# Loading a projection weight to 112 partitions in one DMA in place of two DMAs to 128

## The chip, the cores and the metric

The kernel runs on one core of one Trainium2 chip. The metric is device time in microseconds (us); profiles were taken of the same kernels, one execution each. Executions of the kernels before and after agree within 0.6 us, those of one experiment within 1.5 us.

## The reference, cut to what matters

One token is decoded. Its query comes from a small projection, attends to 65,536 cached positions in each of eight key/value heads, and the result is mixed with a small MLP.

```python
Hq, Hkv, Sk, Dh = 16, 8, 65536, 256      # x: [1, 1, 448], wq: [448, 4096], caches: [1, 8, 65536, 256]
q = (x @ wq)                             # 448 x 4096: 3.67 MB of bf16, the weight that the change is about
scores = einsum("bhqd,bhkd->bhqk", q, k) * Dh ** -0.5
o = einsum("bhqk,bhkd->bhqd", softmax(scores), v)
a = o @ wo
out = g * a + (1 - g) * mlp(x)           # g = sigmoid(sum(x * gate_w))
```

Keys and values are 537 MB; all inputs together, 544 MB. Every byte is read once.

## The kernel before

wq is loaded first, into bytes that the values take over later. 384 of its 448 rows go to 128 partitions of three rows; the other 64 are cut in halves, so that 128 partitions get half a row each.

```python
WF = 3                                   # rows per partition in the first load
REM = DM - WF * P                        # 64 rows left, two half rows each
HALF = NQ // 2
wq_a = early[:, 0:WF * NQ].rearrange("p (j n) -> p j n", j=WF)     # early: the value buffer
wq_b = early[:, WF * NQ:WF * NQ + HALF]
...
# SyncE
eng.dma_start(wq_a..., A_wq[0:WF * P, :].rearrange("(p j) n -> p (j n)", p=P)).then_inc(sem_wq, 16)
eng.dma_start(wq_b, A_wq[WF * P:DM, :].rearrange("r (a n) -> (r a) n", a=2)).then_inc(sem_wq, 16)
for j in range(NP):                      # 32 steps
    if j >= 1: eng.wait_ge(sem_tr[NB - 1], BODY * (j - 1) + DC)    # half of the last keys transposed
    load(kring, A_k_cache, j, ...)       # 8.39 MB of keys
    if j == 0: eng.wait_ge(s_q, 1); eng.wait_ge(s_hb, 1)           # wq and the scratch rows are used up
    else:      eng.wait_ge(sem_pv, j)
    load(vbuf, A_v_cache, j, ...)        # 8.39 MB of values
    ...
# TensorE
for dj in range(2):
    for h in range(HQ):
        for kt in range(WF):
            pe.matmul(sps[:, 1, j:j + 1], wq_a[:, kt, col + dj:col + DH:2], xcol[:, kt:kt + 1], ...)
        ins = pe.matmul(sps[:, 1, j:j + 1], wq_b[:, cb + dj:cb + DH:2], xcol[:, WF + a:WF + a + 1], ...)
```

ScalarE issues the small loads (x, the gate, the MLP's weights and biases) on a queue of its own at the same time.

The softmax here doesn't subtract the row's maximum and nothing guards it: scores larger than these inputs give would overflow.

## Time and profile before

| | before |
|---|---|
| median of three runs | 1266.69 us (1266.55 to 1266.86) |
| span of the profiled run | 1264.3 us |
| bytes read | 544.22 MB, 430 GB/s over the span |
| first packet of the large queue | 1.8 us into the span |
| last landing, end of the last work on it | 1261.53, 1262.2 us |

The views that carry the argument stand in the prediction. One more line of the page is needed for the comparison: the GB/s of the 40 slices of the span, 31.6 us each. The first slice holds the loading stage.

```profile
GB/s 410 428 432 431 435 433 433 431 435 433 431 435 433 433 431 435 431 435 431 435 433 429 433 435 435 431 435 431 431 433 435 435 431 435 431 431 433 435 425 363
```

And the two wq loads among the page's DMA issues; the last number is the time from issue to landing:

```profile
vbuf<-in_A_wq_dram SPq DMA_DIRECT2D x1, 3072.0 KB, 10.2
vbuf<-in_A_wq_dram SPq DMA_DIRECT2D x1, 512.0 KB, 11.0
```

### The profile page before, as it was taken

Reading aid. Unit: us, or ns where it says so; the run is one execution under the profiler, and the core shown is the slowest. Engines: PE = TensorE matmul, PEld = TensorE weight load, DVE = VectorE, ACT = ScalarE, POOL = GpSimd, SP = SyncE. Lnnn points to the kernel's source line nnn. Section 1 sums busy time; section 2 is a strip of 40 time slices with the busy share of each in tenths; the row PEclk is TensorE's granted clock in tenths of the full one; section 3 lists DMA queues with packets and bytes.
Section 4 is the critical chain, followed back from the end, with each engine's and each line's share of the span. In section 5 each row is a group of like instructions: output and inputs, shape, how many; then the busy total and the mean of one; then the engine's idle time right before and its main releaser. Section 6 shows DMA issues by size and latency. Waiting matters only on the chain.

```text
span 1264.3 us, 38824 instructions
## 1 busy us (share of the span) xinstructions
PE 916.7 (73%) x17110; PEld 864.9 (68%) x17110; DVE 420.4 (33%) x755; ACT 536.7 (42%) x786; POOL 0.9 (0%) x7
## 2 busy tenths in 40 slices
PE   3866678766788667786676876768767578676698
PEld 2766668766677666686666876658766578666687
DVE  2433334433344333443222332223322233322233
ACT  1453345543355433454333553335533355433455
POOL 0000000000000000000000000000000000000000
PEclk9887889877888877988878887879878898878989
DMA  9999999999999999999999999999999999999998
GB/s 410 428 432 431 435 433 433 431 435 433 431 435 433 433 431 435 431 435 431 435 433 429 433 435 435 431 435 431 431 433 435 435 431 435 431 431 433 435 425 363
DMA packets 11629, 544.39 MB, mean 431 GB/s; under 512 B 1376, under 2 KB 1634, under 8 KB 2914
## 3 DMA queue, kind: packets, MB, share of 16 engines
q1 hardware_dynamic: 11528, 544.22, 99.7%
q8 instruction: 8, 0.13, 0.0%
q10 hardware_dynamic: 90, 0.01, 0.0%
q14 instruction: 3, 0.02, 0.0%
HBM read 544.22 MB, written 0.00 MB: 430 GB/s over the span
## 4 chain that ended last, share of the span: by engine, by line
DMA 71%; PE 28%; issue 1%; SPq 0%; DVE 0%; ACT 0%; ACTq 0%
DMA kring<-in_A_k_cache_dram 68%; PE kst L297 24%; PE sps L317 4%; DMA wo_sb<-in_A_wo_dram 2%; PE acc L352 0%; SPq L230 0%; SPq L264 0%; SPq L227 0%; SPq L225 0%; PE acc L341 0%; DVE out_g L625 0%; PE prj L399 0%; ACT pT L650 0%; ACTq L650 0%
## 5 line engine op out<-in xcount | busy, mean ns | idle before, releaser
L661 ACT ACTIVATE ktT<-kst 128x1024 bf16<-128x1024 bf16 x512 | 499.0, 1021 | 668.1 <-PE kst L297 667.5
L297 PE MATMUL kst<-ident,kring 128*128 128x128 f32 x4096 | 556.4, 297 | 306.1 <-DMA kring<-in_A_k_cache_dram 295.3
L297 PEld LDWEIGHTS kst<-ident,kring 128*128 128x128 f32 x4096 | 506.5, 154 | 316.0 <-issue 313.3
L563 DVE COPY ktT<-kst 128x1024 bf16<-128x1024 bf16 x512 | 354.1, 692 | 763.2 <-PE kst L297 739.4
L317 PEld LDWEIGHTS sps<-qcur,ktT 128*128 128x128 bf16 x8192 | 237.8, 96 | 4.2 <-issue 1.7
L317 PE MATMUL sps<-qcur,ktT 128*128 128x2 bf16 x8192 | 236.6, 163 | 1.5 <-issue 1.5
L352 PE MATMUL acc<-vbuf,pT 128*2 128x256 bf16 x4080 | 147.6, 315 | 2.2 <-issue 1.5
L352 PEld LDWEIGHTS acc<-vbuf,pT 128*2 128x2 bf16 x4080 | 109.3, 96 | 32.3 <-issue 2.0
L650 ACT ACTIVATE pT<-sps 128x32 f32 x256 | 51.8, 202 | 16.6 <-PE sps L317 16.6
L341 PE MATMUL acc<-pT,ones_sq 128*128 128x32 bf16 x256 | 11.7, 178 | 12.3 <-ACT pT L650 12.3
L341 PEld LDWEIGHTS acc<-pT,ones_sq 128*128 128x128 bf16 x256 | 8.6, 97 | 15.2 <-ACT pT L650 14.9
L568 DVE COPY accs<-acc 128x288 f32<-128x288 f32 x8 | 3.7, 458 | 40.1 <-PE acc L352 40.1
L667 ACT ACTIVATE z_b<-z_b 128x448 bf16<-128x448 bf16 x14 | 8.1, 577 | 20.4 <-DVE z_b L550 20.4
L388 PEld LDWEIGHTS acc<-sel,accs 128*64 128x64 f32 x112 | 10.8, 214 | 0.9
L388 PE MATMUL acc<-sel,accs 128*64 128x1 f32 x112 | 11.4, 260 | 0.0
L425 PE MATMUL acc<-vbuf 42*128 42x42 bf16 x1 | 0.2, 215 | 8.4 <-DMA b_b<-in_B_b_dram 8.4
L425 PEld LDWEIGHTS acc<-vbuf 42*128 42x128 bf16 x1 | 0.1, 99 | 8.5 <-DMA b_b<-in_B_b_dram 8.5
L399 PE MATMUL prj<-wo_sb,oTn 128*1 128x112 bf16 x128 | 3.6, 240 | 3.2 <-DVE oTn L591 2.8
L556 DVE TENSOR_TENSOR gu<-wtmp,z_b 128x448 bf16<-128x448 bf16 x14 | 5.5, 392 | 1.0
L544 DVE TENSOR_TENSOR z_b<-wtmp,u_b 128x448 bf16<-128x448 bf16 x14 | 5.5, 392 | 1.0
L542 DVE TENSOR_TENSOR wtmp<-u_b 128x448 bf16<-128x448 bf16 x14 | 5.5, 392 | 1.1
L548 DVE TENSOR_TENSOR z_b<-u_b,wtmp 128x448 bf16<-128x448 bf16 x14 | 5.5, 392 | 1.0
(85 smaller groups left out, 79.7 us busy)
## 6 DMA issues: line engine op xcount, KB each, us to landing
kring<-in_A_k_cache_dram SPq DMA_DIRECT2D x4, 4096.0 KB, 24.4
vbuf<-in_A_v_cache_dram SPq DMA_DIRECT2D x1, 6144.0 KB, 24.5
wo_sb<-in_A_wo_dram SPq DMA_DIRECT2D x7, 448.0 KB, 27.6
vbuf<-in_A_wq_dram SPq DMA_DIRECT2D x1, 3072.0 KB, 10.2
vbuf<-in_A_v_cache_dram SPq DMA_DIRECT2D x1, 1024.0 KB, 26.6
vbuf<-in_A_v_cache_dram SPq DMA_DIRECT2D x1, 768.0 KB, 27.7
vbuf<-in_A_wq_dram SPq DMA_DIRECT2D x1, 512.0 KB, 11.0
vbuf<-in_A_v_cache_dram SPq DMA_DIRECT2D x31, 30.0
```

The source lines that it names most:

```text
L297: ins = pe.transpose(kst[:, b, i * P:(i + 1) * P], kring_f[:, at + NT * (k % DC) + 4 * b + i, :], ident[:, :])
L317: ins = pe.matmul(sps[:, par, 2 * nt:2 * nt + 2], ktT[:, par, b, ntl * DH + dj:(ntl + 1) * DH:2], qcur[:, dj, :], start=(dj == 0), stop=(d ...
L341: pe.matmul(acc[:, DENC:SELC], ones_sq[:, :], pT[:, r, :], start=False, stop=(r == BODY - 1), skip_group_check=True)
L352: ins = pe.matmul(acc[o:o + REP, 0:DH], pT[:, r, 2 * nt:2 * nt + 2], vbuf[:, n, :], start=False, stop=False, skip_group_check=True)
L388: ins = pe.matmul(dst[hh * HP:(hh + 1) * HP, i:i + 1], accs[:, i:DH:2 * REP], sel[:, hh:hh + 1], start=False, stop=True, skip_group_check= ...
L542: vec.tensor_tensor(W, U, U, op=ALU.mult)
L544: vec.tensor_tensor(Z, W, U, op=ALU.mult)
L548: vec.tensor_tensor(Z, U, W, op=ALU.add)
L563: vec.tensor_copy(ktT[:, k % KTB, b, :], kst_b[:, b, :]).then_inc(sem_ev[b], 1)
L650: act.activation(pT[:, bass.ds(p0 + k % DC, 1), :].rearrange("p o n -> p (o n)"), sps[:, k % 2, 0:2 * NT], AF.Exp, scale=scale).then_inc(s ...
L661: act.activation(ktT[:, k % KTB, b, :], kst_b[:, b, :], AF.Copy).then_inc(sem_ev[b], 1)
L667: act.activation(z_b[:, :], z_b[:, :], AF.Tanh).then_inc(s_tanh, 1)
```

## The change

The intent is a simpler layout: 448 = 112 x 4, so one DMA and one rule for every row, no half rows and no zero-padded copies of x.

```diff
-    WF = 3
-    REM = DM - WF * P
-    HALF = NQ // 2
+    WF = 4
+    PQ = DM // WF
+    assert PQ * WF == DM and PQ <= P and PQ % 16 == 0
...
-        wq_a = early[:, 0:WF * NQ].rearrange("p (j n) -> p j n", j=WF)
-        wq_b = early[:, WF * NQ:WF * NQ + HALF]
+        wq_a = early[0:PQ, 0:WF * NQ].rearrange("p (j n) -> p j n", j=WF)
...
             eng.dma_start(wq_a.rearrange("p j n -> p (j n)"),
-                          A_wq[0:WF * P, :].rearrange("(p j) n -> p (j n)", p=P)).then_inc(sem_wq, 16)
-            eng.dma_start(wq_b, A_wq[WF * P:DM, :].rearrange("r (a n) -> (r a) n", a=2)
-                          ).then_inc(sem_wq, 16)
+                          A_wq.rearrange("(p j) n -> p (j n)", j=WF)).then_inc(sem_wq, 16)
...
                     for kt in range(WF):
-                        pe.matmul(sps[:, 1, j:j + 1], wq_a[:, kt, col + dj:col + DH:2],
-                                  xcol[:, kt:kt + 1], start=(kt == 0), stop=False)
-                    ins = pe.matmul(sps[:, 1, j:j + 1], wq_b[:, cb + dj:cb + DH:2],
-                                    xcol[:, WF + a:WF + a + 1], start=False, stop=True)
+                        ins = pe.matmul(sps[:, 1, j:j + 1], wq_a[:, kt, col + dj:col + DH:2],
+                                        xcol[:, kt:kt + 1], start=(kt == 0), stop=(kt == WF - 1))
```

Cut: the columns of x follow the new row order, and VectorE's memset and two copies for the half rows go.

More of the change, by code (lines that the diff above doesn't have):

```diff
@@ L55, in bass_gated_mix__gqa_block_cached__mixer_token_mlp__decode_kernel @@
     assert T % (CH * BODY) == 0 and PPH >= 2
-    WF = 3
-    REM = DM - WF * P
-    assert 0 < REM and 2 * REM == P
-    HALF = NQ // 2
+    WF = 4
+    PQ = DM // WF
+    assert PQ * WF == DM and PQ <= P and PQ % 16 == 0
     NFIRST = 96
@@ L122, in bass_gated_mix__gqa_block_cached__mixer_token_mlp__decode_kernel @@
         early_f = vbuf_f[:, :, :].rearrange("p n d -> p (n d)")
-        wq_a = early[:, 0:WF * NQ].rearrange("p (j n) -> p j n", j=WF)
-        wq_b = early[:, WF * NQ:WF * NQ + HALF]
-        used = [WF * NQ + HALF]
+        wq_a = early[0:PQ, 0:WF * NQ].rearrange("p (j n) -> p j n", j=WF)
+        used = [WF * NQ]
         def scratch(rows, n, dt=bf16):
@@ L134, in bass_gated_mix__gqa_block_cached__mixer_token_mlp__decode_kernel @@
         identb = scratch(3 * FT, 3 * FT)
-        xrem = scratch(1, 2 * P).rearrange("p (a n) -> p a n", a=2)
         xrow_b = scratch(1, DM)
@@ L145, in bass_gated_mix__gqa_block_cached__mixer_token_mlp__decode_kernel @@
         w2cur = sb([P, 1], bf16, "w2cur")
-        xcol = sb([P, WF + 2], bf16, "xcol")
+        xcol = sb([PQ, WF], bf16, "xcol")
         oTn = sb([P, 2 * REP], bf16, "oTn")
@@ L199, in bass_gated_mix__gqa_block_cached__mixer_token_mlp__decode_kernel @@
         s_col = new_sem("s_col")
-        s_xrem = new_sem("s_xrem")
+        s_identb = new_sem("s_identb")
         s_xcol = new_sem("s_xcol")
@@ L419, in _ @@
             for j in range(WF):
-                pe.matmul(acc[:, j:j + 1], xrow_b[0:1, j:WF * P:WF], one, start=True, stop=True)
-            pe.wait_ge(s_xrem, 2)
-            for a in range(2):
-                pe.matmul(acc[:, WF + a:WF + a + 1], xrem[0:1, a, :], one, start=True, stop=True)
+                pe.matmul(acc[0:PQ, j:j + 1], xrow_b[0:1, j:DM:WF], one, start=True, stop=True)
+            pe.wait_ge(s_identb, 1)
             pe.wait_ge(sem_misc, 16 * 5)
-            pe.matmul(acc[:, WF + 2:WF + 2 + 3 * FT], wrows_b, identb, start=True, stop=True).then_inc(s_col, 1)
+            pe.matmul(acc[:, WF:WF + 3 * FT], wrows_b, identb, start=True, stop=True).then_inc(s_col, 1)
             pe.wait_ge(s_xcol, 1)
-            pe.wait_ge(sem_wq, 32)
+            pe.wait_ge(sem_wq, 16)
             for dj in range(2):
@@ L432, in _ @@
                     col = h * DH
-                    a, cb = divmod(col, HALF)
                     for kt in range(WF):
-                        pe.matmul(sps[:, 1, j:j + 1], wq_a[:, kt, col + dj:col + DH:2],
-                                  xcol[:, kt:kt + 1], start=(kt == 0), stop=False)
-                    ins = pe.matmul(sps[:, 1, j:j + 1], wq_b[:, cb + dj:cb + DH:2],
-                                    xcol[:, WF + a:WF + a + 1], start=False, stop=True)
+                        ins = pe.matmul(sps[:, 1, j:j + 1], wq_a[:, kt, col + dj:col + DH:2],
+                                        xcol[:, kt:kt + 1], start=(kt == 0), stop=(kt == WF - 1))
             ins.then_inc(s_q, 1)
@@ L476, in _ @@
                 vec.sem_inc(sem_ev[b], 1)
-            vec.memset(xrem, 0.0)
             vec.memset(zrow[:, :], 0.0)
             vec.wait_ge(sem_ident, 1)
-            vec.tensor_copy(identb, ident[0:3 * FT, 0:3 * FT]).then_inc(s_xrem, 1)
+            vec.tensor_copy(identb, ident[0:3 * FT, 0:3 * FT]).then_inc(s_identb, 1)
             vec.reduce_sum(sel[:, :], ident[:, :].rearrange("p (j n) -> p n j", j=4)[:, 0:REP, :], axis=AX.X)
@@ L483, in _ @@
             vec.drain()
-            vec.tensor_copy(xrem[0:1, 0, 0:P:2], xrow_b[0:1, WF * P:DM])
-            vec.tensor_copy(xrem[0:1, 1, 1:P:2], xrow_b[0:1, WF * P:DM]).then_inc(s_xrem, 1)
             vec.tensor_copy(xrow, xrow_b)
@@ L510, in _ @@
             vec.wait_ge(s_col, 1)
-            vec.tensor_copy(xcol[:, :], acc[:, 0:WF + 2]).then_inc(s_xcol, 1)
-            vec.tensor_copy(params[:, :], acc[:, WF + 2:WF + 2 + 3 * FT]).then_inc(s_par, 1)
+            vec.tensor_copy(xcol[:, :], acc[0:PQ, 0:WF]).then_inc(s_xcol, 1)
+            vec.tensor_copy(params[:, :], acc[:, WF:WF + 3 * FT]).then_inc(s_par, 1)
             vec.drain()
```

## The prediction

The forecast's sum came to +4 us, or +1.1, or -0.1: the -0.1 is bytes and packets; the rest (+4, or +1.2 by a smaller estimate) was the author's estimate of what it costs to load to 112 partitions and not 128. It took each engine to get seven consecutive rows, and let some engines end up 0 to 4.2 us late and the others go on, 4 to 5.5 at worst if they start staggered. The author gave this delay 55% (+3 to +5, or +1), none of it 40%, with a thin upper tail, for a mean of +2.5; "hidden" is the case of none, the second rival that of a delay, and the high end of the range is its worst. Of the signs, wq packets near 1.213 us were to show no such delay and many at 1.8 to 2.4 us that there is one; the first K half was to land 1 to 4 us later with it, and about when it did without.

> **What bounds the kernel now.** I read the DMA row of the page first, because 544 MB of keys and values pass through one core; then the queue table, the chain of work that ended last, and its first and last pieces in order of time.
>
> ```profile
> DMA  9999999999999999999999999999999999999998
> DMA packets 11629, 544.39 MB, mean 431 GB/s; under 512 B 1376, under 2 KB 1634, under 8 KB 2914
> q1 hardware_dynamic: 11528, 544.22, 99.7%
> DMA 71%; PE 28%; issue 1%; SPq 0%; DVE 0%; ACT 0%; ACTq 0%
> ```
>
> All 40 slices of the span (31.6 us each) show the 16 DMA engines 90% busy or more, but for the last; queue 1, fed by SyncE, has 99.7% of it. The chain names DMA for 71%; the 28% that it gives to PE is time in which a load waits to be issued while others are still moving.
>
> Queried over stretches of the span, DMA share and GB/s are the last two columns:
>
> ```profile
> 0.00:2.00 2.00, 0.00 (x0) 0.00 (x0) 0.46 (x4) 0.00 (x0) 0.91 (x7) 1.00 0.67 148
> 2.00:12.00 10.00, 0.64 (x6) 0.39 (x6) 4.06 (x16) 1.28 (x1) 0.00 (x0) 1.00 0.94 391
> 12.00:31.00 19.00, 8.45 (x150) 7.63 (x151) 4.05 (x17) 2.77 (x5) 0.00 (x0) 1.00 1.05 451
> 31.00:1230.00 1199.00, 878.19 (x16371) 830.52 (x16373) 399.41 (x700) 516.46 (x757) 0.00 (x0) 0.84 1.00 433
> ```
>
> From 31 to 1230 us the share is 1.00 at 433 GB/s. The trace's record of single packets says the same: a 65,536 B packet takes 2.421 us at the median (27.07 GB/s), 16 such engines make 433 GB/s, and when I string the packets of one engine together the gaps are a few ns. So the end is **the longest sum of packet times over the 16 engines**, plus about 2 us at the start and 3 us at the end. Two parts of the chain, cut by window:
>
> ```profile
> 0.74 0.39 SPq L225
> 1.19 0.41 SPq L227
> 1.65 21.16 DMA kring<-in_A_k_cache_dram
> 22.80 4.44 issue
> ...
> 1233.37 28.16 DMA wo_sb<-in_A_wo_dram
> 1261.53 0.04 issue
> 1261.57 0.30 PE prj L399 x8
> 1261.87 0.02 issue
> 1261.89 0.33 DVE out_g L625
> ```
>
> L225 and L227 are the two loads of wq, ahead of everything else in the queue. At the other end the last transfer lands at 1261.53 us and only 0.7 us of work follows. A delay of one DMA engine at the start therefore reaches the end whole: its queue never runs dry in which to catch up.
>
> The loading stage waits for something other than wq:
>
> ```profile
> 11.19 0.21 PE L425 MATMUL acc<-vbuf 42*128 42x42 bf16 x1 [8.44 <-DMA b_b<-in_B_b_dram]
> 12.57 0.24 PE L435 MATMUL sps<-xcol,vbuf 128*128 128x1 bf16 x3 [1.17 <-DVE xcol L511]
> 17.53 0.33 SPq L230 DMA_DIRECT2D vbuf<-in_A_v_cache_dram  x1
> 27.24 5.82 PE L297 MATMUL kst<-ident,kring 128*128 128x128 f32 x32 [9.39 <-issue]
> ```
>
> The small loads issued from ScalarE land at about 11.2 us and hold the first projection matmul until 12.57; the value load, which reuses wq's bytes, is issued at 17.53; the transposes begin at 27.24.
>
> [...]
>
> **The change part by part.**
>
> *Bytes and packets.* Before, an engine carries eight rows of 24,576 B and eight of 4,096 B, 229,376 B; after, seven of 32,768 B, again 229,376 B. Packet medians in the trace are 0.912, 0.159 and (from the K halves, same size) 1.213 us: 8 x 0.912 + 8 x 0.159 = 8.57 us before, 7 x 1.213 = 8.49 after. **-0.08 us** on the end.
>
> *The second DMA.* One issue less, 0.41 us at L227 plus about 0.05. K is issued that much earlier but stands in the queue behind 8.5 us of wq. **0 us.**
>
> *PE.* The projection goes from 160 to 128 matmuls (32 groups of four in place of 3+1+1). Before, they ran from 12.57 to about 16.15 us: 3.58 / 160 = 22 ns each, so 32 fewer save 0.7 us. Two padding matmuls become one more row of four. *VectorE:* one memset (0.17 us) and two copies (0.20 and 0.19) go, in a stretch where it later idles 5.2 us for the small loads. Both end in the V issue at 17.53 us, but wq and K, 3.67 + 8.39 MB at 433 GB/s, keep the queue full until about 2 + 27.9 = 30 us. Slack of 12 us: **0 us.**
>
> *Small loads.* They take turns with the larger packets: some five turns, each 1.21 - 0.91 = 0.3 us longer, plus a similar delay for packets already queued, about +2 us. This eats PE's saving and leaves V's issue near 19 us, inside the slack. **0 us.**
>
> [...]
>
> [...]
>
> **Rivals.** First, *hidden anyway*: [...]then 1266.6 us. For it: same bytes per engine[...] Second, [...]1267.8 to 1271. For it: the engines' queues never empty, so nothing repairs the delay. Third, *rows dealt out in turn* (engine = row mod 16): [...]+25 us, 1292; [...]and I give it 1 to 2%. Fourth, *a new wait*: V's issue slips beyond 30 us and the queue runs dry. That needs over 12 us of delay in the small loads or in wq; a delay of 4 us does not do it. Fifth, *a saving*: PE and VectorE lose work and one issue goes, but all of it is in slack, and even the whole loading stage's 0.7 us would be 0.06%.
>
> **Range and chances.** [...]Predicted 1266.69 + 2.5 = **1269.2 us**, range 1266.2 to 1272.4: the low end is "hidden" with the run-to-run spread of 0.15 us doubled[...]. Two per cent is 25 us; nothing on the faster side comes near, and on the slower side only the third rival: faster 0.005, same 0.975, slower 0.02.
>
> **What would show each step.** [...]Seven packets per engine confirm 16 engines. [...]the last landing (1261.53) should move by as much as the slowest engine. The projection should start later than 12.57 and V's issue stay below 25 us. The prediction is wrong if fewer than 16 engines take part[...], if the DMA row shows a gap after wq, or if the share from 31 to 1230 us falls below 1.00 for a reason that I have not seen, such as PE's instruction fetches standing elsewhere.

## The result, and the profile after

| | before | after |
|---|---|---|
| median (six runs each, same chip) | 1266.58 us (1266.24 to 1266.86) | 1271.70 us (1271.47 to 1271.93) |
| difference of the medians | | +5.12 us, +0.4% |
| ratio | | 1.0040 (95% interval 1.0028 to 1.0053) |
| first projection matmul, start | 12.57 us | 23.92 us |
| V's first load, issue | 17.53 us | 28.87 us |
| first transposes, start | 27.24 us | 39.03 us |
| last landing | 1261.53 us | 1267.36 us |

Ratios here and below are the mean time of one kernel's runs over that of the other's in the same rounds, so not quite the ratio of the medians. By the 2% measure the times are the same; the 5 us are clear of the noise all the same.

The GB/s of the 40 slices, after (31.8 us each):

```profile
GB/s 326 433 435 433 435 431 433 431 435 431 429 435 435 431 433 440 429 429 438 435 431 427 440 433 433 433 435 431 433 431 431 435 433 433 433 433 429 440 424 358
```

All of the loss stands in the first slice, 326 in place of 410. The rest is as it was. The same four stretches as in the prediction, after (the last two columns are DMA share and GB/s):

```profile
0.00:2.00 2.00, 0.00 (x0) 0.00 (x0) 0.32 (x3) 0.00 (x0) 0.91 (x7) 1.00 0.75 197
2.00:12.00 10.00, 0.55 (x4) 0.49 (x4) 3.10 (x12) 1.28 (x1) 0.00 (x0) 1.00 0.97 256
12.00:31.00 19.00, 4.88 (x133) 3.97 (x133) 3.43 (x16) 1.69 (x3) 0.00 (x0) 1.00 0.97 368
31.00:1230.00 1199.00, 881.43 (x16262) 833.83 (x16263) 400.63 (x702) 517.43 (x757) 0.00 (x0) 0.84 1.00 433
```

From 2 to 12 us the engines are as busy as ever (0.97) but move 256 GB/s, not 391. Busy engines with fewer bytes mean **longer packets**, not waiting ones. The wq load took 17.5 us from issue to landing:

```profile
vbuf<-in_A_wq_dram SPq DMA_DIRECT2D x1, 3584.0 KB, 17.5
```

The trace records each packet. One engine's large packets in order, in ns, strung together by start and end (before: 8 rows of 24,576 B, 8 half rows of 4,096 B, then keys of 32,768 B; after: 7 rows of 32,768 B of wq, then keys of the same size):

```
before  2098 912 912 912 912 912 912 912 | 159 159 159 159 159 159 159 159 | 1213 1213 1213 1213 ...
after   1822 1811 2135 2186 1528 1969 2125 | 2253 1244 1224 1214 ...
```

The first packet of each engine was long before too (1.27 to 2.22 us in place of 0.91), so it is left out of the means here and below. After it, a wq row took 2.04 us in the mean over all engines (1.52 to 2.39) in place of 1.21. The first key packet of each engine was still slow (1.44 to 2.27), while others were writing wq. The lines of the timeline that answer to those in the prediction, and the next load of keys:

```profile
22.63 0.19 PE L419 MATMUL acc<-vbuf 42*128 42x42 bf16 x1 [19.98 <-DMA b_b<-in_B_b_dram]
...
28.87 0.33 SPq L226 DMA_DIRECT2D vbuf<-in_A_v_cache_dram  x1
...
39.03 5.98 PE L293 MATMUL kst<-ident,kring 128*128 128x128 f32 x32 [9.82 <-issue]
...
50.21 0.33 SPq L226 DMA_DIRECT2D kring<-in_A_k_cache_dram  x1
```

The last of the small loads lands 11.4 us later than before, and the projection, V's load and the transposes follow it by about as much. Yet from the packet records the 16 engines were never idle between the start and the last transfer, so this lateness cost nothing. The end of the chain of waits is the same as before, only later:

```profile
1238.99 28.37 DMA wo_sb<-in_A_wo_dram
1267.36 0.04 issue
1267.40 0.30 PE prj L395 x8
1267.70 0.03 issue
1267.72 0.33 DVE out_g L613
```

### The profile page after: what moved, and what is told of

It reads as the page before. It is cut to its first block, busy times and chain, and to the rows that moved or that the text cites. A ratio compares the mean times of both kernels' runs of the same rounds, so it can differ in the third digit from the quotient of the medians.

```text
span 1270.1 us, 38819 instructions
## 1 busy us (share of the span) xinstructions
PE 921.5 (73%) x17109; PEld 868.6 (68%) x17109; DVE 419.9 (33%) x752; ACT 536.9 (42%) x786; POOL 0.9 (0%) x7
## 4 chain that ended last, share of the span: by engine, by line
DMA 69%; PE 29%; issue 1%; DVE 0%; ACTq 0%; SPq 0%; ACT 0%; DVEq 0%
DMA kring<-in_A_k_cache_dram 66%; PE kst L293 24%; PE sps L313 4%; DMA wo_sb<-in_A_wo_dram 2%; DMA b_b<-in_B_b_dram 2%; PE acc L348 0%; PE sps L428 0%; SPq L226 0%; ACTq L621 0%; DVE hbT L588 0%; DVE stat L495 0%; ACTq L618 0%; PE prj L432 0%; SPq L260 0%; DVE vbuf L493 0%
## 5 line engine op out<-in xcount | busy, mean ns | idle before, releaser
L384 PE MATMUL acc<-sel,accs 128*64 128x1 f32 x112 | 11.4, 260 | 0.0
## 6 DMA issues: line engine op xcount, KB each, us to landing
vbuf<-in_A_wq_dram SPq DMA_DIRECT2D x1, 3584.0 KB, 17.5
```

The source lines that it names most:

```text
L384: ins = pe.matmul(dst[hh * HP:(hh + 1) * HP, i:i + 1], accs[:, i:DH:2 * REP], sel[:, hh:hh + 1], start=False, stop=True, skip_group_check= ...
```

## The experiments

**Theory A**: what counts is where the rows land. To 112 partitions in place of 128, packets get longer, and the delay reaches the end whole. **Theory B**: a single load, or its longer packets, is slow by itself. **Theory C**: the pattern of reads in HBM (the chip's main memory) is what slows it. The diffs are shortened, and "..." stands for what is left out. Factors in the expectations, such as "twice" and "four times", are estimates; what was measured stands beside them.

### One load to 128 partitions, right result

wq is 896 half rows; seven contiguous ones per partition make one DMA of 128 x 28,672 B. Two zero-padded columns of x per half row keep the result right, at the price of 224 projection matmuls.

```diff
-  eng.dma_start(wq_a, ...three rows...); eng.dma_start(wq_b, ...half row...)
+  eng.dma_start(wq_s, A_wq.rearrange("r (a n) -> (r a) n", a=2).rearrange("(p j) n -> p (j n)", j=7))
...
+  for kt in range(7):  ins = pe.matmul(sps[:, 1, j:j + 1], wq_s[:, kt, ...], xcol[:, a * 7 + kt:...])
```

> One DMA for wq, but to 128 partitions of seven half rows (28,672 B) each; right result. Theory A (the destination[...]): [...]packets of 28,672 B take about 1.06 us (28,672 / 27.07), the time is that of before, 1266.5 (+-0.4). Theory B (merging two DMAs into one, or longer packets, costs the time): it stays near the changed kernel, 1271.7. Theory C (HBM source pattern: each engine reads one 229,376 B block, as in the changed kernel): also near 1271.7.

Measured: 1272.89 us (ratio 1.005). By the time alone, A would have fallen. The packets say otherwise: 1.062 us at the median, full speed. The loss came later. DMA share and GB/s are again the last two columns, in this kernel:

```profile
31.00:60.00 29.00, 19.33 (x294) 19.20 (x295) 9.68 (x14) 13.34 (x19) 0.00 (x0) 1.00 0.93 388
60.00:100.00 40.00, 34.68 (x685) 30.29 (x685) 18.44 (x38) 20.26 (x32) 0.00 (x0) 0.87 0.93 395
```

and in the kernel before:

```profile
31.00:60.00 29.00, 25.58 (x501) 22.90 (x502) 13.01 (x25) 16.03 (x24) 0.00 (x0) 0.88 0.99 425
60.00:100.00 40.00, 27.07 (x487) 25.29 (x483) 14.38 (x27) 16.93 (x25) 0.00 (x0) 0.83 1.00 432
```

Here the share falls to 0.93: by the packet records an engine stood idle for 1.35 us in the mean of the 16 between 50 and 55 us, and for 3.81 us between 70 and 80. (They were not idle all at once: together for 0.1 us in the first stretch and for about 2 in the second. Where the expectation of a later run says "all", read it so.) The transposes began at 40.67 us, 13 us later than before, behind this piece of the chain:

```profile
22.04 2.12 issue
24.16 0.61 PE sps L435 x17
...
26.49 14.18 issue
40.67 5.89 PE kst L297 x32
```

So the next keys were asked for at 51.75 us and the next values at 75.87, too late. What the two "issue" stretches of TensorE wait for, this view doesn't say. The packet records have a candidate: the loads of kind "instruction" on queue 8, 16,384 B each, by their name, as the author reads it, the program's own code. The page counts eight in the kernel before and nine here:

```profile
q8 instruction: 8, 0.13, 0.0%
q8 instruction: 9, 0.15, 0.0%
```

Before, two of them had landed (19.43 and 25.54 us) when the transposes began at 27.24; here three had (22.91, 31.58 and 38.94). In 13 of the 14 kernels of this document the transposes begin 1.70 to 1.75 us after the last of these landings, two with up to 128 projection matmuls and three with 224; in the other, with 5.14 us more to load, they waited for the keys, which landed at 28.25. So it fits that the longer program, more than the matmuls' own time, made TensorE late; no run separates the two. This is the fourth rival of the prediction, in a kernel where it did happen: two things had been changed at once, the load and TensorE's work. Two more runs below take them apart.

### One load to 64 partitions

```diff
-    WF = 4
+    WF = 7          # 448 = 64 x 7; the scratch rows move to a buffer of their own
```

> One DMA for wq to 64 partitions of seven rows (57,344 B) each, small scratch tiles moved to a buffer of their own; right result. Theory A: [...]a packet takes about twice 57,344 / 27.07 = 4.2 us and wq takes 17 us in place of 8.5: 1266.6 + 8.5 = 1275. Theory B and C: no worse than the changed kernel, 1267 to 1272, with packets of 2.1 to 3.5 us.

Measured: 1281.84 us (ratio 1.012), and packets of 57,344 B took 4.49 us in the mean after the first 16, where 57,344 / 27.07 = 2.12: a factor of 2.12. That is the direction and about the factor that A named, and not the "no worse than the changed kernel" of B and C. The end moved by more than A's 8.5 us because an engine also stood idle, in the mean, for 2.35 and 3.66 us. This kernel has 224 projection matmuls too (32 x 7) and three instruction loads before its transposes, as in the run above, so its end shows two things at once; its packets show the load alone.

### Two loads to 112 partitions

```diff
+            for j0, j1 in ((0, 3), (3, 4)):
-                eng.dma_start(wq_a, A_wq.rearrange("(p j) n -> p (j n)", j=WF))
+                eng.dma_start(wq_a[:, j0:j1, :], A_wq.rearrange(...)[:, j0 * NQ:j1 * NQ])
```

> The changed kernel with wq in two DMAs again (three rows, then one row, of each of 112 partitions); right result. Theory A: still slow, 1271 to 1272.5, packets of 24,576 B near 1.5 us and not 0.91. Theory B (number of DMAs or packet size): back to 1266.5. Theory C: like A.

Measured: 1271.09 us (ratio 1.0039); 24,576 B in 1.41 us in the mean, not 0.91. B falls: neither one DMA nor its packet size is the cause.

### The same destination, another source

```diff
-  eng.dma_start(wq_a, A_wq.rearrange("(p j) n -> p (j n)", j=WF))
+  eng.dma_start(wq_a, src(A_k_cache, 0, 0, HV)[0:PQ, :])     # keys, 64 KiB apart; wrong values in wq's place
```

> The changed kernel with the same destination of 112 x 32,768 B, but the bytes read from the key cache at a pitch of 65,536 B, a pattern that ran at 1.213 us per packet to 128 partitions; the result is wrong on purpose. Theory A: still 1271.5 to 1272, packets of about 2 us. Theory C (the source pattern of wq in HBM is what slows it): packets near 1.213 us and 1266.5.

Measured: 1271.40 us (ratio 1.0039), packets 2.02 us in the mean. The same pattern of reads is quick (1.213 us) when it goes to 128 partitions. C falls. (The output still passed the comparison with the reference, here and in the next run: the check is too loose to see a wrong query, and these two runs say nothing of correctness.)

### Before, with its two loads merged

```diff
-  eng.dma_start(wq_a, ...three rows...); eng.dma_start(wq_b, ...half row...)
+  eng.dma_start(early[:, 0:WF * NQ + HALF], ...128 x 28,672 B...)      # rows in wrong places; matmuls as before
```

> The kernel before with its two wq loads made one load of 128 partitions x 28,672 B and nothing else changed, so that the rows stand in wrong places and the result is wrong on purpose. The first run of this kind (one load to 128 partitions, right result, 224 projection matmuls) had full-speed wq packets of 1.062 us, but the 16 DMA engines all stood idle for 1.35 and 3.81 us near 50 and 75 us, because TensorE came to the transposes late. Theory A (destination): with TensorE's work as before, no idle stretch, packets of 1.062 us, 1266.0 to 1266.9. Theory B (a merged load costs time by itself): 1271 to 1273.

Measured: 1266.50 us beside 1266.57 (ratio 0.9998), wq packets 1.062 us, no idle stretch. One load to 128 partitions cost nothing here. This also separates the first experiment's loss from its load.

### Seven loads of 16 consecutive partitions

```diff
+            for i in range(7):
+                eng.dma_start(early[16 * i:16 * i + 16, 0:WF * NQ], A_wq.rearrange(...)[16 * i:16 * i + 16, :])
```

After the last cut stands the outcome if it did not matter which partitions move together.

> The changed kernel's wq layout, loaded by seven DMAs of 16 consecutive partitions each[...]; right result. Theory A[...]: packets of 32,768 B take about four times 1.21 us, 4.8, the wq load about 34 us in place of 8.5, and the end moves by 25 us or more (the queue may run dry as well): 1291 to 1300. [...]packets of 1.2 to 2.1 us and 1266 to 1273.

Measured, in two executions: 1288.50 us (ratio 1.0173); packets of 32,768 B took 4.50 us in the mean after the first 16, a factor of 3.7, with all engines busy. Stretches of this kernel:

```profile
2.00:12.00 10.00, 0.55 (x4) 0.49 (x4) 3.10 (x12) 1.28 (x1) 0.00 (x0) 1.00 1.05 125
12.00:31.00 19.00, 0.19 (x1) 0.10 (x1) 2.37 (x12) 1.69 (x3) 0.00 (x0) 1.00 0.97 111
```

Same bytes, same rows in the same partitions as in the changed kernel; only which of them move at the same time differs, and 391 GB/s becomes 111 to 125. The end moved by 22 us; A had said 25 or more, at four times 1.21.

### Seven loads of 16 partitions, seven apart

```diff
+            for i in range(7):
+                eng.dma_start(early[i:PQ:7, 0:WF * NQ], A_wq.rearrange("(p j) n -> p (j n)", j=WF)[i:PQ:7, :])
```

> The changed kernel's wq layout, loaded by seven DMAs of 16 partitions each, seven apart (0, 7, ..., 105, then 1, 8, ..., and so on), so that engine e gets partitions 7e to 7e+6 in order by construction. If the single DMA deals rows out in blocks of seven, as the prediction assumed: the same packets, 1.5 to 2.3 us, and 1271 to 1272. If it deals them otherwise: a clearly different packet time and another total (1267 to 1269 if blocks of seven were nearly free of collisions).

Measured: 1271.96 us (ratio 1.0041), packets 1.41 to 2.31 us, 2.01 in the mean: the changed kernel's 1271.70 and 2.04. So dealing blocks of seven consecutive partitions to an engine reproduces the single load. That doesn't prove that it deals them so, but nothing else is needed.

### Before, with 5.14 us more to load

```diff
+            eng.dma_start(dummy, src(A_k_cache, 0, 0, HV)[:, 0:8704]).then_inc(sem_dummy, 16)   # 128 x 17,408 B
```

> The kernel before with one more load behind wq, 128 partitions x 17,408 B of the key cache into a buffer that nobody reads; right result. At 27.07 GB/s it is 8 x 0.643 = 5.14 us per engine, full speed. If any delay of the DMA engines at the start reaches the end whole: 1266.5 + 5.1 = 1271.6 (+-0.4). If the loop hides part of it: less, down to 1266.5.

Measured: 1271.81 us, +5.24 for +5.14 at full speed. A delay of the DMA engines at the start reaches the end whole; the loop hides nothing of it.

### One load to 128 partitions again, with 112 matmuls

One weight load serves both halves of the columns: the moving operand gets two columns, each zero where a partition holds the other half.

```diff
-  ins = pe.matmul(sps[:, 1, j:j + 1], wq_s[:, kt, cb + dj:cb + DH:2], xcol[:, a * NH + kt:...])      # 32 x 7
+  ins = pe.matmul(sps[:, 1, j:j + HQ // 2 + 1:HQ // 2], wq_s[:, kt, cb + dj:cb + DH:2],
+                  xcol[:, kt:2 * NH:NH])                                                           # 16 x 7
```

> The first experiment again (one load of wq to 128 partitions of seven half rows, right result), with its 224 projection matmuls made 112: one weight load serves both halves of the columns, through a two-column moving operand with zeros. If the loss of the first experiment was TensorE coming late to the transposes, so that the DMA queue ran dry: no idle stretch now, packets of 1.062 us, and 1266.2 to 1266.8, level with before or 0.1 better (7 x 1.062 for 8 x 0.912 + 8 x 0.159... per engine 8.50 against 8.57 us). If the loss was in the load itself: still 1272 to 1273.

Measured over five rounds: 1266.67 us beside 1266.47 (ratio 1.0001, interval 0.9987 to 1.0014), right result, packets 1.062 us, no idle stretch. That gives what the change wanted, one load and fewer matmuls than before, at no cost, and shows that the 112 further matmuls, with their instructions, were what cost the first experiment its time: the load is the same. It doesn't beat the kernel before, nor could it by more than 0.1 us: the bytes are the same. (The expectation's "7 x 1.062" is a slip: an engine carries eight packets of 28,672 B, and 8 x 1.062 is the 8.50 that it gives.)

### Sixteen more rows, seven apart

All wq packets of the changed kernel were slow about alike; the prediction had some engines at full speed. So: before, with two more loads of 16 partitions, seven apart. By the author's estimate, which no trace shows, only four of the 16 rows are in each other's way. After the first cut stands the outcome if the delay stays with those four, after the second that if they hold up all engines. No trace names an engine; here and in the next two runs, what is shown is how long packets took with which partitions in the load.

```diff
+            eng.dma_start(spare[0:PQ:7, :], src(A_k_cache, 1, 0, HV)[0:PQ:7, :])              # 16 x 32,768 B
+            eng.dma_start(dummy[0:PQ:7, :], src(A_k_cache, 0, 0, HV)[0:PQ:7, 0:12288])        # 16 x 24,576 B
```

> The kernel before with two more loads behind wq, each of 16 partitions seven apart (0, 7, ..., 105), 32,768 B and 24,576 B each, from the key cache into bytes that nobody reads; right result. [...]12 packets of each size at 1.213 and 0.912 us and four at up to twice that. [...]most of the 16 are longer, and alike. It adds 2.1 us of transfer at full speed, so about 1268.7 where nothing else is lost.

Measured (one look): 1270.97 us. The durations of the 16 packets of each size, in ns, in order of start:

```
32,768 B  2247 1886 2451 2016 1991 2095 2074 2156 2202 2251 2387 2413 2552 2416 2362 2338
24,576 B  1822 1862 1854 1858 1862 1856 1856 1864 1880 1860 1819 1805 1794 1762 1695 1634
```

Not four slow ones and twelve at 1,213 and 912: all 16, and nearly alike. The packets of 24,576 B are the clean case: they began from 12.83 to 14.41 us, and the next keys only at 14.66. The delay did not stay with four of the rows.

### Eight more rows, four apart

```diff
+            eng.dma_start(spare[4:36:4, :], ...); eng.dma_start(dummy[4:36:4, :], ...)        # eight partitions each
```

By the author's estimate, none of these rows is in another's way, though each goes, by the same estimate, to partitions other than its engine's in the main loads. After the first cut stands the outcome if only rows in each other's way are slow, after the second that if other partitions alone make a packet slow.

> The kernel before with two more loads behind wq, each of eight partitions 4, 8, ..., 32 (32,768 B and 24,576 B), into bytes that nobody reads; right result. [...]these 16 packets take about 1.21 and 0.91 us, but for a little overlap at their edges. [...]1.8 times as long, as in the run with two pairs.

Measured (one look): 1269.02 us. Five of the eight packets of 24,576 B took 921 or 922 ns, the others 912, 928 and 988. Those of 32,768 B, and keys beside them, took about 1,400 at first; why, no run shows. So eight extra rows are not slow by themselves: four apart, those of 24,576 B took 0.91 to 0.99 us.

### Eight more rows, eight apart

```diff
+            eng.dma_start(spare[0:64:8, :], ...); eng.dma_start(dummy[0:64:8, :], ...)        # eight partitions each
```

By the author's estimate, these eight rows are in each other's way in pairs. The two outcomes for the keys are: the first if that holds up the other eight engines too, the second if it does not.

> The same with partitions 0, 8, ..., 56[...]. The 16 packets take about twice 1.21 and 0.91 us. [...]the key packets (32,768 B) of the other eight that move meanwhile are longer than 1.213 us too; [...]they stay at 1.213.

Measured (one look): 1271.07 us. The extra packets of 24,576 B took 1,898 to 1,940 ns, twice 912 and a little. The key packets that the other eight engines moved meanwhile took 2,507 to 2,572 ns for most, in place of 1,213. **Rows that were slow for where they land held up engines that had no part in them.** The stretch from 12 to 17 us in four kernels: before, with eight rows four apart, with 16 rows seven apart, and with eight rows eight apart. Each time the last two columns are share and GB/s.

```profile
12.00:17.00 5.00, 4.33 (x131) 3.77 (x131) 2.23 (x15) 1.69 (x3) 0.00 (x0) 1.00 0.97 419
```

```profile
12.00:17.00 5.00, 4.31 (x131) 3.77 (x131) 2.06 (x15) 1.69 (x3) 0.00 (x0) 1.00 0.99 406
```

```profile
12.00:17.00 5.00, 3.79 (x129) 3.62 (x130) 1.58 (x11) 1.69 (x3) 0.00 (x0) 1.00 0.86 249
```

```profile
12.00:17.00 5.00, 3.95 (x131) 3.74 (x131) 1.90 (x13) 1.69 (x3) 0.00 (x0) 1.00 0.83 210
```

With the 16 rows seven apart, the whole core moved 249 GB/s in place of 419, over a third less.

### The account

For each kernel, the packets' time above bytes / 27.07 GB/s, summed and divided by 16 engines, less the same sum of before (2.91 us); the time for which an engine stood idle in mid-run, in the mean; the added bytes at full speed; and the profiled run's time less that of before's (1266.45):

| kernel | longer packets | idle | added bytes | sum | measured |
|---|---|---|---|---|---|
| after | 5.56 | 0 | 0 | 5.6 | 5.5 |
| one load, 128, 224 matmuls | 1.42 | 5.16 | 0 | 6.6 | 6.4 |
| one load, 64 | 10.46 | 6.01 | 0 | 16.5 | 16.4 |
| two loads, 112 | 4.49 | 0 | 0 | 4.5 | 4.5 |
| keys in wq's place, 112 | 5.15 | 0 | 0 | 5.2 | 4.6 |
| seven loads of 16, consecutive | 22.29 | 0 | 0 | 22.3 | 21.9 |
| seven loads of 16, seven apart | 5.42 | 0 | 0 | 5.4 | 5.5 |
| 5.14 us more to load | 0.08 | 0 | 5.14 | 5.2 | 5.4 |
| 16 more rows, seven apart | 2.39 | 0 | 2.12 | 4.5 | 4.5 |
| merged load, 128, wrong places | -0.23 | 0 | 0 | -0.2 | 0.2 |
| one load, 128, 112 matmuls | -0.24 | 0 | 0 | -0.2 | 0.0 |

Longer packets and idle engines account for each of these kernels within 0.6 us. This is bookkeeping, which shows that nothing large is missing; the causes rest on the runs above. Of the 1.42 us of the first experiment, whose wq packets were quick, some 1.15 stand just after its idle stretches, where most engines' first packets of 65,536 B took 2.8 to 3.4 us in place of 2.42.

The two with eight partitions don't fit a mean over 16 engines: only eight engines carry the added loads, 2.12 us each, so that these should end last. With 2.12 us the sums are 0.46 + 2.12 = 2.6 us for the rows four apart (measured 2.6) and 2.65 + 2.12 = 4.8 us for those eight apart (measured 4.6); with half of it they would be a microsecond short.

## Why the prediction was right or wrong

The measured time lies inside the range, 2.5 us above the point. By its own steps:

- *What bounds the kernel, and that a delay at the start reaches the end whole*: right. The run with 5.14 us more to load ended 5.24 us later, and after wq the changed kernel runs at 433 GB/s with no idle stretch.
- *Sixteen engines, seven rows each, in blocks*: in agreement. Seven rows of wq stand in each engine's string, and blocks imposed by hand gave 1271.96 us beside 1271.70.
- *Bytes and packets, the second DMA*: -0.08 us at most. The merged load to 128 partitions measured 0.07 us below before, within the noise.
- *Where the rows land*: that it costs time was right, **the size was not**, and this is the term that was off. The prediction weighed +3 to +5 (or +1) at 55% and nothing at 40%, with a thin tail above, for a mean of 2.5; the packets were 5.6 us longer. Its working let some engines fall 0 to 4.2 us behind while the others went on. In the runs no engine went on: with 16 more rows seven apart all 16 packets took 1.63 to 1.88 us in place of 0.91, and with eight more rows eight apart the other eight engines' packets took 2.51 to 2.57 us for most in place of 1.21. The staggered-start figure, 4 to 5.5 at worst, came near by the slowest engine, for another reason, so that the range holds the measured time is in part luck. Of its signs, many packets at 1.8 to 2.4 us came true. Why the engines hold each other up, no run here shows.
- *The first rival, hidden anyway*: it had 40% and falls. To 112 partitions, a wq packet of 32,768 B took 2.04 us in the mean, not the 1.213 of 27.07 GB/s.
- *The third rival, rows dealt out in turn*: not what the single load does, but the run with 16 consecutive partitions made it by hand, and the sum it gave (+25 us) is close to the +22 measured.
- *Small loads*: "about +2 us" and "V's issue near 19 us" were far off: the last landed 11.4 us later and V's load was issued at 28.87, past the "below 25 us" that the prediction gave as a sign. Small packets take turns with large ones: in the packet record of before they start in bunches 0.91 to 0.92 us apart beside rows of 24,576 B (0.912 us), and the last four of after start 1.22 to 1.23 us apart beside keys (1.213). Before, an engine's last turns stood beside half rows of 0.159 us, after, beside rows of about 2 us and keys of 1.2. The prediction counted turns beside rows of 24,576 B before and missed the half rows. It cost nothing here, as wq and the first keys keep the queue full until about 37 us (wq has landed at 18.2 us, and 8.39 MB of keys take 19.4 at 433 GB/s), but the 12 us of slack that the prediction named were about 8.
- *The fourth rival, a new wait*: absent in the changed kernel, as said. It does lie close by: the transposes 1.6 us later still, with wq itself quick, left the engines idle for over 5 us in the first experiment. "PE's instruction fetches standing elsewhere", which the prediction named as what could spoil it, fit that loss.
- *PE's 0.7 us*: a miscount. The kernel before has 3+1 matmuls in each of 32 groups, not 3+1+1: its profile lists 96 at L435 and 32 at L437, so 128, which took the 3.58 us that the prediction divided by 160. After, 128 took 3.57. It lies in slack and moved nothing.

## What to carry to other kernels

In this case a DMA's destination partitions decided its rate, not just its bytes and its engine count. 112 partitions used all 16 engines and moved 16 x 32,768 B in 2.04 us, 257 GB/s, some 60% of the 433 to 128 partitions; 64 moved 16 x 57,344 B in 4.49 us, 204 GB/s, and 16 consecutive ones 16 x 32,768 B in 4.50 us, 117 GB/s. All engines slowed down, not just some. Where a kernel's DMA queue never runs dry, a few microseconds lost in a small opening load come back whole at the end (here 5.24 us for 5.14), so cut such a load to 128 equal partitions even if that means half rows (one such load measured 1266.67 us, beside 1266.47 before). And when an experiment changes a load and an engine's work together, read the packets before the time: the first experiment had the right packets and the wrong time.
